# Two FNet + GLU layers on one core: the second layer's DFT over columns folded once more, and the row tests spread anew

## The chip, the cores and the metric

The kernel runs on one core of one Trainium2 chip. The metric is the device time of one execution in microseconds (us); less is better. Three timed runs of the kernel before gave 1104.46 to 1105.48 us, with a median of 1104.56. The execution that the profiler recorded took 1106.03 us, 1.47 us above that median; its span in the trace, from the first to the last recorded instruction, is 1104.2 us.

## What is computed

Two equal layers work on x, 2048 rows of 640 columns. Each layer first mixes (the real part of a DFT over the columns and a DFT over the rows, by products with given matrices), then applies a gated feed-forward part with F = 1728; both add to x and both begin with a row normalization.

```python
def _A_ref(x, dft_seq_re, dft_seq_im, dft_hid_re, dft_hid_im):
    a = jnp.einsum("bsd,ed->bse", x, dft_hid_re)
    b = jnp.einsum("bsd,ed->bse", x, dft_hid_im)
    return jnp.einsum("ts,bse->bte", dft_seq_re, a) - jnp.einsum("ts,bse->bte", dft_seq_im, b)

def _B_ref(x, w_gate, w_up, w_down):
    g = jnp.einsum("bsd,df->bsf", x, w_gate)
    u = jnp.einsum("bsd,df->bsf", x, w_up)
    return jnp.einsum("bsf,fd->bsd", _sigmoid(g) * u, w_down)

for layer in range(2):
    x = x + _A_ref(_layernorm(x), dft_seq_re, dft_seq_im, dft_hid_re, dft_hid_im)
    x = x + _B_ref(_layernorm(x), w_gate, w_up, w_down)
```

The DFT matrices are inputs like all others. The kernel uses their symmetries and so also tests, row by row, that what it was given has them; if a test fails, a general version runs instead.

## The kernel before

**Arithmetic.** x stays in SBUF for the whole run. Every large product of fp32 numbers is done as three products of fp16 halves (high by high, high by low, low by high), so one "matmul" of the mathematics is three matmuls on TensorE, each with a weight load of its own.

**Folding.** Because of the symmetries of a DFT, rows s, S-s, S/2-s and S/2+s are added and subtracted in quads before the product, and so are columns c and 640-c. Half of the columns are left, EC = 321 of them for the even sums ("e") and 320 for the odd ones ("o"). For the second layer this fold runs on VectorE (DVE) beside the first layer's last stages, quad by quad (four quads, 0 to 3): `fold_columns` (L593, L594), `fold_double` (L600), `fold_rows` (L636, L642), and `fold_join` (L675 to L682). In `fold_join` the last sums are formed on DVE (L675), copied to fp16 by ScalarE (ACT, L677), and the low half is left by a subtraction on DVE (L682). Quads 0 to 2 are done ahead; quad 3 needs the first layer's very last rows and so is finished while the second layer's first products already run.

**The start of the second layer** ("he" in the code) is a list of steps: eight `sequence` steps, the DFT over rows of quad i for the even (EV) or odd (OD) outputs (matmuls at L796, and L800 for one odd row), eight `hidden` steps and one `hidden_middle`, the DFT over columns (`product`, matmuls at L922). A `sequence` step fills three PSUM banks over two quads; `evict_sums` takes them out, ACT the high half (L237) and DVE the low half (L239). A `hidden` step is 18 matmuls of 321 columns into two banks; they come out through `evict_hidden` on ACT (L961, L971) or DVE (L966). There are eight banks in all, given out in the order in which they came free. After these steps x is normalized, transposed on TensorE (L540, 20 matmuls each), and the feed-forward part begins at the mark "b0" with `gate_up` (L1130).

**The feed-forward part** works in two halves of the rows. For each, gate blocks (`seven` and `four`, matmuls of 512 columns at L1174) run over the 13 tiles of F, and then `stage` steps (L1430, L1411) multiply by `w_down`. In a gate block six products of one tile follow one another on TensorE: one, five, two, six, (four of the tile before), three, seven, 45 to 54 matmuls together. Four of the results are copied out of PSUM by ACT (`snap`, L1178); "six" may start only when "one" was copied, and "seven" only when "six" was. ACT also does the sigmoids (L1181). The transposes of the normalized rows that feed the gate blocks are DMA transposes issued by SyncE (SP, L533).

**Row tests.** 100 of them, each with a load into a "room" of SBUF (4 DMAs of 128 KB for `load_rows`, L1502), one to four DVE instructions (`test_rows`, L1509 and L1511) and a squared sum on ACT (`square_sum`, L1481). Three rooms are used in turn. A table `spans` gives each stretch of the run a weight, and the tests are spread by it.

**What sets the order.** Nothing is scheduled at run time. `steps` is TensorE's order with a planned duration for each step; `when(t, ...)` and `run(step, ...)` put the other engines' work at planned times or steps, and each engine takes its own instructions in that order. `PLACES` is a list of SBUF addresses, one for each buffer in the order in which buffers are taken; which buffer reuses which place, and so which instruction must wait for which, follows from it. All DMAs but a few gathers are issued by SP.

## Time and profile before

| | |
|---|---|
| median of three timed runs | 1104.56 us |
| the profiled execution's own time | 1106.03 us |
| its span in the trace | 1104.2 us |
| TensorE (PE) busy | 98% of the span |
| VectorE (DVE) / ScalarE (ACT) / GpSimd (POOL) busy | 75% / 52% / 14% |
| start of the second layer (first L796 to first `gate_up`) | 571.66 to 612.46 us |
| second layer's first gate block, its stages | about 652.8 to 780 us, 780 to 852 us |
| second layer's last gate block, its stages | 860 to 1018 us, 1018 to 1098 us |

How to read it: the profile gives for each engine the time in which it did something, and, for each stretch in which it did nothing, the instruction whose end let it go on. With TensorE at 98% a time can only fall much if TensorE's own work falls, or if one of the few stretches goes in which it waits. A row of a timeline or of the chain reads: start, duration, engine and line, and xN for N instructions.

### The profile page before, as it was taken

What the parts mean: (1) busy time and instruction counts of PE and PEld (TensorE: products, weight loads), DVE (VectorE), ACT (ScalarE), POOL (GpSimd) and SP (SyncE); (2) the same over time, 40 slices, a digit from 0 to 9 for tenths busy, and PEclk for the clock granted to TensorE, in tenths of its full rate; (3) what the DMA queues carried; (4) which work ended last, traced back from release to release, by engine and by line L of the source; (5) the groups of instructions that cost most, each with busy time, mean ns of one, the idle gap of its engine ahead of it and who ended that gap; (6) DMA issues with size and microseconds to landing.
All of it is one profiled execution on the core that took longest, in us unless ns stands there. A gap on an engine that the chain in (4) does not pass through costs nothing.

```text
span 1104.2 us, 17528 instructions
## 1 busy us (share of the span) xinstructions
PE 1084.0 (98%) x6289; PEld 626.3 (57%) x6289; DVE 830.2 (75%) x1608; ACT 572.9 (52%) x1109; POOL 154.6 (14%) x250
## 2 busy tenths in 40 slices
PE   6999999999999999999999999999999999999997
PEld 3776444457774444457777844444677444444775
DVE  8996789868448999769887569895895356777962
ACT  7776547765315665555225544476761345555520
POOL 3110153312333151000110100012000010000010
PEclk9999999999999999999999999999999999999999
DMA  8414765366996877756742058645569856666521
GB/s 273 155 61 71 199 184 203 115 193 191 251 249 233 251 250 202 235 174 214 229 141 73 1 62 194 200 154 182 185 163 177 265 180 208 202 196 194 190 88 64
DMA packets 183079, 194.70 MB, mean 176 GB/s; under 512 B 76451, under 2 KB 145474, under 8 KB 182982
## 3 DMA queue, kind: packets, MB, share of 16 engines
q1 hardware_dynamic: 182342, 190.87, 58.8%
q0 software_dynamic: 640, 2.62, 0.6%
q8 instruction: 51, 0.84, 0.3%
q14 instruction: 46, 0.38, 0.1%
HBM read 145.29 MB, written 31.91 MB: 160 GB/s over the span
## 4 chain that ended last, share of the span: by engine, by line
PE 87%; DVE 8%; issue 2%; DMA 1%; ACT 1%; POOL 0%; SPq 0%; DVEq 0%; POOLq 0%; ACTq 0%
PE acc L1174 36%; PE acc L1430 17%; PE acc L1130 14%; PE acc L1316 8%; PE acc L922 4%; PE acc L1411 2%; PE acc L1283 2%; PE acc L834 2%; DVE big L642 1%; DMA big<-big 1%; DVE quad L424 1%; DVE big L239 1%; PE acc L796 1%; DVE big L1509 1%; DVE big L594 0%
## 5 line engine op out<-in xcount | busy, mean ns | idle before, releaser
L1174 PE MATMUL acc<-big 128*128 128x512 f16 x2160 | 467.8, 379 | 2.8 <-ACT big L1178 1.9
L1174 PEld LDWEIGHTS <-big 128*128 128x128 f16 x2160 | 211.3, 98 | 257.8 <-issue 3.5
L1430 PE MATMUL acc<-big 128*128 128x320 f16 x1512 | 213.2, 299 | 0.4 <-DVE big L1304 0.4
L1178 ACT ACTIVATE big<-acc 128x512 f32<-128x512 f32 x160 | 94.0, 593 | 191.9 <-PE acc L1174 167.5
L1430 PEld LDWEIGHTS <-big 128*128 128x128 f16 x1512 | 147.9, 98 | 58.5 <-issue 0.6
L1130 PE MATMUL acc<-big 128*128 128x512 f16 (+1 forms) x900 | 156.6, 336 | 0.0
L1130 PEld LDWEIGHTS <-big 128*128 128x128 f16 x900 | 87.9, 98 | 67.7 <-DVE big L239 0.2
L1481 ACT ACTIVATE big<-big 128x768 f32<-128x768 f32 (+6 forms) x106 | 79.0, 745 | 53.2 <-DVE big L1511 17.0
L1304 DVE SCALAR_TENSOR_TENSOR big<-acc,big 128x320 f32<-128x320 f32 x112 | 53.1, 485 | 53.7 <-PE acc L1411 27.2
L239 DVE SCALAR_TENSOR_TENSOR big<-big 128x640 f16<-128x640 f32 (+7 forms) x94 | 75.9, 830 | 22.5 <-ACT big L237 19.4
L1316 PE MATMUL acc<-big 128*128 128x320 f16 x656 | 89.3, 299 | 0.0
L1391 DVE TENSOR_TENSOR big<-big 128x512 f16<-128x512 f32 x126 | 85.3, 688 | 2.3 <-ACT big L1390 2.3
L1390 ACT ACTIVATE big<-big 128x512 f16<-128x512 f32 x126 | 74.0, 618 | 25.0 <-DVE big L1391 11.1
L237 ACT ACTIVATE big<-big 128x640 f16<-128x640 f32 (+9 forms) x94 | 63.8, 707 | 35.7 <-POOL big L1082 15.8
L1316 PEld LDWEIGHTS <-big 128*128 128x128 f16 x656 | 64.2, 98 | 25.1
L1224 DVE TENSOR_TENSOR big<-big,acc 128x512 f32<-128x512 f32 x40 | 27.3, 682 | 44.4 <-PE acc L1174 30.6
L516 ACT ACTIVATE big<-big 128x384 f16<-128x384 f32 (+2 forms) x56 | 36.0, 667 | 36.6 <-DVE big L501 17.2
L1181 ACT ACTIVATE big<-big 128x512 f32<-128x512 f32 x80 | 49.7, 622 | 9.7 <-DVE big L1224 6.6
L386 POOL DMA_INDIRECT out<-big,rows x8 | 8.6, 1070 | 310.9 <-DVE big L1304 173.5
L1509 DVE TENSOR_TENSOR big<-big 128x512 f32<-128x512 f32 x64 | 46.2, 722 | 5.9 <-DMA big<-in_ct 5.7
L1402 DVE TENSOR_TENSOR big<-big 128x512 f32<-128x512 f32 x72 | 50.1, 697 | 0.1
L439 POOL TENSOR_SCALAR rowt<-rowt 128x1 f32<-128x1 f32 x24 | 13.0, 540 | 242.4 <-ACT big L437 242.4
(199 smaller groups left out, 1230.2 us busy)
## 6 DMA issues: line engine op xcount, KB each, us to landing
big<-in_ct SPq DMA_DIRECT2D x256, 128.0 KB
big<-kept_f SPq DMA_DIRECT2D x63, 320.0 KB
big<-kept_S SPq DMA_DIRECT2D x33, 512.0 KB
big<-kept_w SPq DMA_DIRECT2D x33, 320.0 KB
big<-in_ct SPq DMA_DIRECT2D x32, 256.0 KB
big<-kept_G SPq DMA_DIRECT2D x21, 320.0 KB
kept_S<-big SPq DMA_DIRECT2D x13, 512.0 KB
big<-in_wg SPq DMA_DIRECT2D x19, 320.0 KB
```

The source lines that it names most:

```text
L237: nc.scalar.activation(dh, src, AF.Copy, scale=s)
L239: nc.vector.scalar_tensor_tensor(dl, src, s, dh, op0=OP.mult, op1=OP.subtract)
L1130: nc.tensor.matmul(ps, w[wp][:, d * P : (d + 1) * P], xt[:, xp, :], start=(d == 0 and wp == HI and xp == HI), stop=(d == ND - 1 and wp == LO))
L1174: nc.tensor.matmul(ps, wt, xt, start=start and n == 0, stop=n == len(todo) - 1, skip_group_check=not start)
L1178: nc.scalar.activation(dst, ps, AF.Copy)
L1304: nc.vector.scalar_tensor_tensor(xe, ps[:, :EH], CB, xe, op0=OP.mult, op1=OP.add)
L1316: nc.tensor.matmul(held["pd", i, e][0][:, :EH], held["t", half, j].parts[hp][:, i * P : (i + 1) * P], held["w", 2, j].parts[wp][:, e * EH ...
L1390: nc.scalar.activation(h, v, AF.Copy)
L1391: nc.vector.tensor_tensor(l, v, h, op=OP.subtract)
L1430: nc.tensor.matmul(ps[:, :EH], a[n][hp][:, i * P : (i + 1) * P], w[n][:, wp], start=fresh and m == 0, stop=m == len(todo) - 1, skip_group_ ...
L1481: nc.scalar.activation(v, v, AF.Square, accum_out=new_sum()[:p])
L1509: nc.vector.tensor_tensor(bd[:, :, 1], bd[:, :, 0], bd[:, :, 1], op=same)
```

## The change

**1. The second fold.** The columns of the folded sums have one more symmetry, c against 320-c. For the second layer they are folded again: sums in 161 columns, differences in 160 (`fold_again`). In the DFT over columns the first two thirds of the contraction (d = 0, 1) then touch only every other output column, 161 of 322, while the last third (d = 2) keeps all 322. The first layer keeps its way. The scale constants XF and ZS are halved.

```diff
+    def fold_again(to, f, r):
+        c, every = EH - 2 * r, (slice(None),) * (len(f.shape) - 1)
+        for n, to_c, op in ((HE + 1, 0, OP.add), (HE, HE + 1, OP.subtract)):
+            nc.vector.tensor_tensor(to[(*every, slice(to_c, to_c + n))], f[(*every, slice(0, n))],
+                                    f[(*every, slice(c, c - n, -1))], op=op)
...
-    def fold_join(i, v=ALL, do=(0, 1, 2)):
+    def fold_join(i, v=ALL, do=(0, 1, 2, 3), only=ALL):
...
             if 1 in do:
-                nc.scalar.activation(take_parts(key, i)[:, :, 0, :w], f[:, GB::2], AF.Copy)
...
+                fold_again(a, b, n)
             if 2 in do:
-                p = take_parts(key, i)
-                nc.vector.tensor_tensor(p[:, :, 1, :w], f[:, GB::2], p[:, :, 0, :w], op=OP.subtract)
+                nc.scalar.activation(p[:, :, 0, :EC], a, AF.Copy)
+            if 3 in do:
+                nc.vector.tensor_tensor(p[:, :, 1, :EC], a, p[:, :, 0, :EC], op=OP.subtract)
...
     def product(ps, ph, r, at, m):
-        for d, (_, n) in enumerate(KT[r]):
-            w = held["h", r, d].f16[:n]
+        for d, (_, n) in enumerate(KT):
+            o = ps[:m, : EC + 1 if steps else EC]
+            if steps and d < 2:
+                c = (r + d) % 2
+                o = ps[:m, c * (HE + 1) : (c + 1) * (HE + 1)]
```

**2. Its weights.** Before, the fp16 DFT weights of the opening were stored (six DMAs) and loaded again (`load_wh_again`, planned 60 us after the first layer's last stages begin). Now the fp32 rows that are needed are loaded (`load_wh2`, planned 4 to 14 us after that point) and split again on ACT, DVE and, for a column of zeros, POOL (`split_wh2`). Eleven DVE instructions on 128x1 and 128x4 numbers in the opening (`hs2`) prepare their factors.

**3. The order at the start of the second layer.** The steps and the evictions between them are listed anew, and quad 3's join is cut in two halves with evictions ahead of and between them.

```diff
             order = [(sequence, 0, EV), (sequence, 1, EV), (sequence, 0, OD), (sequence, 1, OD), (sequence, 2, EV),
-                     (sequence, 2, OD), (hidden, 0, 0), (sequence, 3, EV), (hidden, 1, 0), (sequence, 3, OD),
-                     (hidden, 0, 1), (hidden, 2, 0), (hidden, 3, 0), (hidden, 1, 1), (hidden, 2, 1), (hidden, 3, 1),
-                     (hidden_middle,)]
+                     (sequence, 3, EV), (sequence, 2, OD), (hidden, 0, 0), (hidden, 0, 1), (sequence, 3, OD),
+                     (hidden, 1, 0), (hidden, 1, 1), (hidden, 2, 0), (hidden, 3, 0), (hidden_middle,),
+                     (hidden, 2, 1), (hidden, 3, 1)]
...
-    run_at(end + 3, [(fold_join, 3, ALL, (n,)) for n in range(3)])
...
-    run(he + 2, evictions(0, (EV,)))
+    join = [[(fold_join, 3, ALL, (n,), (k,)) for n in range(1, 4)] for k in range(2)]
+    run(he + 2, [(evict_sums, 0, EV, 0), (fold_join, 3, ALL, (0,)), *join[0], *evictions(0, (EV,))[1:], *join[1]])
     run(he + 4, evictions(0, (OD,)))
```

VectorE's rows of the layer's start, before: the end of quad 3's join (L675 joins, L682 leaves the low halves), then the evictions of the first sums (L239, one row for each PSUM bank acc).

```order
780 L675 TENSOR_TENSOR big_60<-big_60 128x321 x2
781 L675 TENSOR_TENSOR big_60<-big_60 128x320 x2
782 L682 TENSOR_TENSOR big_60<-big_60 128x2x321
783 L682 TENSOR_TENSOR big_60<-big_60 128x2x320
784 L239 SCALAR_TENSOR_TENSOR big_60<-acc6_314,big_60 128x512
785 L239 SCALAR_TENSOR_TENSOR big_60<-acc2_66,big_60 128x512
786 L239 SCALAR_TENSOR_TENSOR big_60<-acc5_313,big_60 65x512
```

The same place in the changed kernel, on the same engine (L241 is the eviction, L699 the join, L684 the second fold, L708 the low half).

```order
785 L241 SCALAR_TENSOR_TENSOR big_60<-acc6_326,big_60 128x512
786 L699 TENSOR_TENSOR big_60<-big_60 128x321 x2
787 L699 TENSOR_TENSOR big_60<-big_60 128x320 x2
788 L684 TENSOR_TENSOR big_60<-big_60 128x161
789 L684 TENSOR_TENSOR big_60<-big_60 128x160
790 L684 TENSOR_TENSOR big_60<-big_60 128x161
791 L684 TENSOR_TENSOR big_60<-big_60 128x160
792 L708 TENSOR_TENSOR big_60<-big_60 128x321 x2
793 L241 SCALAR_TENSOR_TENSOR big_60<-acc2_66,big_60 128x512
794 L241 SCALAR_TENSOR_TENSOR big_60<-acc5_325,big_60 65x512
```

The first eviction stands ahead of the join now, the second and third between its two halves; the second half of the join (four more L684 and two more L708) follows them, ahead of the evictions of the odd sums.

**4. The row tests.** There are 102 (two new ones for the second symmetry, `load_hidden_fold`). Their table names a distance between tests for each stretch instead of a weight. Planned counts by stretch, before and now: first layer's first stages and the stretch behind them 5 and 6; first layer's last gate block 19 and 13; first layer's last stages 10 and 4; second layer's opening `gate_up` block 0 and 6; first gate block of the second layer's first half 24 and 14; its stages 5 and 0; the last gate block 33 and 50; the last stages 4 and 9. In the last gate block there is a fourth room, a test comes three places after its load instead of two, and every other test's row loads are issued by ACT: 21 groups of four DMAs, 128 KB each.

```diff
+            (nc.scalar if apart_rows[0] else nc.sync).dma_start(v[:, g], bass.AP(ct.tensor, (r * S + row) * S, [[256, 8], [d * S, 16], [1, 256]]))
...
+    spans = [(d[0] + 6, d[0] + 38, 7.0), (d[0] + 76, d[1] - 93, 14.0), (d[1] - 43, d[1] - 3, 5.0), (d[1] - 3, d[1] + 47, 12.0),
+             (c - 29, c + 3, 4.5), (c + 60, d2 - 4, 4.8), (j2 + 4, e2, 3.1), (e2, e2 + 45, 5.5)]
...
+        k, wait = (n % 3, 2) if m < 0 else ((3, *((more_rooms + i) % 3 for i in range(3)))[m % 4], 3)
+        when(at_test(n), apart_rows.__setitem__, 0, m >= 0 and m % 2 == 0)
+        when(at_test(n), within, k, load, *key)
+        when(at_test(n + wait), within, k, test, *key)
+        when(at_test(n + wait + 0.85), square_rest)
```

ScalarE's rows in the last gate block, before: copies out of PSUM (L1178), sigmoids (L1181) and the tests' squares (L1481).

```order
747 L1178 ACTIVATE big<-acc_312 128x512
748 L1181 ACTIVATE big<-big 128x512
749 L1481 ACTIVATE big,dsum<-big 128x768
750 L1178 ACTIVATE big<-acc_65 128x512
751 L1481 ACTIVATE big,dsum<-big 128x319
752 L1181 ACTIVATE big<-big 128x512
753 L1178 ACTIVATE big<-acc_65 128x512
```

In the changed kernel the same engine there (L1241 copy, L1244 sigmoid, L1544 square, L1453 a split, L1569 the loads of a row test).

```order
785 L1241 ACTIVATE big<-acc_325 128x512
786 L1244 ACTIVATE big<-big 128x512
787 L1544 ACTIVATE big,dsum<-big 128x768
788 L1241 ACTIVATE big<-acc_324 128x512
789 L1544 ACTIVATE big,dsum<-big 128x768
790 L1569 DMA big<-in_ct 128x1x256 x4
791 L1453 ACTIVATE big<-big 128x512
792 L1244 ACTIVATE big<-big 128x512
```

Four DMA issues stand in ACT's queue behind a square and ahead of the next copies and sigmoids.

SyncE's rows ahead of the second layer's first gate block, before: the eight small DMA transposes of the normalized rows, one after another.

```order
300 L533 DMA_TRANSPOSE big<-big 128x4x128
301 L533 DMA_TRANSPOSE big<-big 128x6x128
302 L533 DMA_TRANSPOSE big<-big 128x4x128
303 L533 DMA_TRANSPOSE big<-big 128x6x128
304 L533 DMA_TRANSPOSE big<-big 128x4x128
305 L533 DMA_TRANSPOSE big<-big 128x6x128
```

In the changed kernel, with eight row loads ahead and four in the midst.

```order
282 L1569 DMA big<-in_ct 128x1x256 x8
283 L542 DMA_TRANSPOSE big<-big 128x4x128
284 L542 DMA_TRANSPOSE big<-big 128x6x128
285 L542 DMA_TRANSPOSE big<-big 128x4x128
286 L542 DMA_TRANSPOSE big<-big 128x6x128
287 L1569 DMA big<-in_ct 128x1x256 x4
288 L542 DMA_TRANSPOSE big<-big 128x4x128
```

The loads of one row test now stand between the fourth and the fifth transpose.

**5. Smaller moves.** In the second layer the normalized rows for the last gate block are applied earlier (18, 42 and 51 planned us after the stages begin instead of 20, 46 and 56), and one of the weight loads behind them (`load_s` of tile 6) is planned 24 instead of 15 us ahead. `PLACES` is a new list throughout; it begins

```diff
-405 80 404 403 81 86 91 96 400 101 395 106 111 116 121 126 390 131 134 384 387 381 140 143 374 369 364 359 354
+405 80 404 81 399 394 389 384 379 81 374 369 364 359 354 349 344 91 94 97 88 341 338 100 105 110 115 330 325
```

231 lines of the change are left out of this document (145 added, 86 removed), and 62 rows, old and new, of the table PLACES.

## The prediction

> **What bounds the kernel now.** I read the page's head, then what TensorE waits for, then the chain of waits at the second layer's start, then busy time by stretch.
>
> The page's head: span, then the engines' busy time.
>
> ```profile
> span 1104.2 us, 17528 instructions
> PE 1084.0 (98%) x6289; PEld 626.3 (57%) x6289; DVE 830.2 (75%) x1608; ACT 572.9 (52%) x1109; POOL 154.6 (14%) x250
> ```
>
> TensorE (PE) is busy for all but 20 us. A change gains by giving it less to do or by ending one of its waits. The waits, by the instruction that ended them (us in total, times, longest):
>
> ```profile
> PE acc L1174 <- ACT big L1178: 1.9, 1, 1.9
> ...
> PE acc L1174 <- DMA big<-big: 0.9, 1, 0.9
> ...
> PE acc L796 <- DVE big L239: 0.6, 1, 0.6
> PE acc L922 <- ACT big L971: 0.5, 1, 0.5
> ```
>
> These four, 3.9 us, are all that lies in places that the change touches; the others stand in the opening and at the first layer's end. The chain at the second layer's start (start, us, engine, line):
>
> ```profile
> 581.24 0.62 DVE big L239
> ...
> 587.15 1.97 PE acc L796 x18
> ...
> 593.55 14.81 PE acc L922 x108
> ...
> 609.62 0.34 ACT big L971
> ...
> 619.18 1.12 PE acc L540 x20
> ```
>
> Between the first and the last of these waits the chain is PE alone: 14.81/108 = 137.1 ns for a matmul of 321 columns, 1.97/18 = 109.4 ns for one of 256, and 1.12/20 = 56 ns for one of 128 columns (a transpose, with its own weight load). All three are the column count by 2.4 per ns and about 3 ns more, so time goes with columns even at 128.
>
> **The second fold: what it removes.** By that line 161 columns cost 161/2.4 + 2.8 = 69.9 ns and 322 cost 137.4 (estimates from those rows). A `hidden` step was 18 x 137.1 = 2.47 us; now it is 12 x 69.9 + 6 x 137.4 = 1.66 us. Nine such steps (with the middle one) give 9 x 0.80 = **-7.2 us** of PE work. The `sequence` steps stay as many and as long. The price for a short matmul has the transposes on one side, and on the other a bound by weight loads:
>
> ```profile
> L922 PEld LDWEIGHTS <-big 128*128 128x128 f16 x96 | 9.3, 97 | 3.6
> L540 PEld LDWEIGHTS <-big 128*128 128x128 f16 x40 | 2.4, 98 | 0.1
> ```
>
> A load shows 97 to 98 ns behind long matmuls and behind the 56 ns transposes alike (40 of them in a busy time of 2.4 us), so these spans overlap and are no cadence. If they were one, a step would be 12 x 98 + 6 x 137.4 = 2.00 us and the gain 9 x 0.47 = 4.2 us. I take 7.2, since the transposes are the nearest row.
>
> [...]
>
> **The second fold: what it gives back.** PE becomes quicker here, and the engines that empty its banks have more to do. The stretch, and DVE's rows in its first part:
>
> ```profile
> 571.66:612.46 40.80, 39.71 (x331) 32.29 (x329) 28.64 (x60) 20.41 (x41) 5.38 (x19) 1.00 0.25 81
> ```
>
> Busy us of PE, PEld, DVE, ACT, POOL follow the length: PE 39.71 of 40.80, the rest being the two waits of 0.6 and 0.5.
>
> ```profile
> 576.90 1.02 DVE L642 SCALAR_TENSOR_TENSOR big<-big,quad 128x321 f32<-128x321 f32 x2 [0.79 <-ACT big L636]
> 577.84 1.69 DVE L675 TENSOR_TENSOR big<-big 128x321 f32<-128x321 f32 x4
> 579.60 1.65 DVE L682 TENSOR_TENSOR big<-big 128x642 f16<-128x642 f32 x2
> 581.16 2.47 DVE L239 SCALAR_TENSOR_TENSOR big<-acc,big 128x512 f16<-128x512 f32 x4
> ...
> 581.90 1.36 PE L796 MATMUL acc<-big 128*65 128x256 f16 x11 [0.56 <-DVE big L239]
> ```
>
> Before, (2,EV)'s third piece waits for a bank because the first L239 stands behind the whole join. Now one L241 is ahead of it, and that wait goes. But the join has eight more L684, of 161 or 160 columns: 0.42 us for 321 in the L675 row, so some 0.24 each, 1.9 us. I laid the new order out from 571.66 with these durations, each engine in its order, an eviction 0.62 on DVE (L239 in the chain):
> - the evictions of (0,OD) come behind the second half of the join, the first of them done at about 585.9; (2,OD) asks for its third bank at about 585.1: +0.8;
> - `hidden` (0,1) follows (0,0) at once and wants the sums of (2,EV) and (3,EV); its last third is evicted 0.3 late;
> - `hidden` (2,0) wants a bank that (3,OD)'s eviction frees, which is queued on DVE behind the first rows' joins and statistics: +0.7;
> - `hidden` (3,1) is last now. Its banks come from (2,1)'s evictions on ACT, behind row 3's statistics and the transposes' copies: +1.0, and the transposes ahead of it +0.1.
>
> The sum, 2.9 us, stands against 1.1 before: the stretch ends at 612.46 - 7.2 + 1.8 = 607.0, **-5.5 us**. From both sides: all of them zero gives -8.3 (7.2 and the old 1.1); every one twice as long gives -2.6. Copying results out in the interleaved order (L1027 and on) I count like the plain copies; no row shows it, and at twice the 0.34 of L971 the two evictions on the path would cost 0.7, inside those ends.
>
> The other edits of this part go beside PE. The eleven `hs2` instructions stand ahead of the first L593. Of their kind, twelve go from 2.63 to 3.74, 0.1 us each, so 1.1 in all, and that L593 waited 1.48 anyway; without this cover they would cost 1.1:
>
> ```profile
> 2.63 0.14 DVE L302 TENSOR_SCALAR big<-big 32x1 f32<-32x1 f32 x1
> ...
> 3.60 0.14 DVE L306 TENSOR_SCALAR big<-big 32x1 f32<-32x1 f32 x1
> ...
> 7.48 0.83 DVE L593 TENSOR_TENSOR big<-big 128x640 f32<-128x640 f32 x1 [1.48 <-ACT big L363]
> ```
>
> The weights' loads and splits lie in the first layer's last stages, where DVE loses six tests and gains six splits of 0.6 (as L239). A test costs DVE about 1.2:
>
> ```profile
> 933.76 0.69 DVE L1509 TENSOR_TENSOR big<-big 128x512 f32<-128x512 f32 x1 [0.21 <-DMA big<-in_ct]
> 934.49 0.49 DVE L1511 TENSOR_TENSOR big<-big 128x128 f32<-128x128 f32 x2
> ```
>
> So DVE has less there than before: nothing on PE, and 3.6 us of DVE work if the tests had stayed.
>
> **The two waits that go.** One is in the first layer's last gate block:
>
> ```profile
> 427.31 1.54 DVE L682 TENSOR_TENSOR big<-big 128x642 f16<-128x642 f32 x2
> ...
> 428.97 1.08 ACT L1178 ACTIVATE big<-acc 128x512 f32<-128x512 f32 x2 [2.22 <-DVE big L682]
> ...
> 429.61 1.67 PE L1174 MATMUL acc<-big 128*128 128x512 f16 x7 [1.90 <-ACT big L1178]
> ...
> 332.00:430.00 98.00, 96.10 (x446) 43.47 (x445) 94.58 (x163) 57.47 (x104) 30.91 (x41) 1.00 0.73 237
> ```
>
> A copy on ACT writes to a place that the fold of quad 1 had, and waits for its last reader, L682, late because DVE is full (94.58 of 98). In the new `PLACES` that copy takes a place that was free long before. DVE there gets the second fold of quads 0 and 1, eight L684 of 322 numbers a row (0.42 each, 3.4 us), and loses six tests (7.2): less than before, so no new lateness is due: **-1.9 us** (0 if the lateness finds another victim).
>
> The other wait is for the large DMA transposes ahead of the last gate block:
>
> ```profile
> 850.82 9.21 DMA big<-big
> 860.03 0.04 issue
> 860.07 45.05 PE acc L1174 x208
> ```
>
> The rows behind them are applied 2 to 5 us earlier, no tests load there, and the weight loads now follow the transposes on SP: **-0.9 us** (0 to -0.9).
>
> **A new wait ahead of the first gate block of the second layer.** SP issues the eight small transposes without a gap:
>
> ```profile
> 638.16 11.96 SPq L533 DMA_TRANSPOSE big<-big x8
> ```
>
> They are issued by 650.12, the last landed by about 651.2, and PE wants the first rows at the block's start, about 652.8, and the last some 1.3 us later: 2.9 us of room for the last. Four L1569 now stand between them, at 0.6 each (row below) 2.4 us, and the new tests delay DVE's part of the rows by 1.6: **+1.1 us** (0 to 2.5, twice that delay).
>
> **ScalarE as an issuer in the last gate block.** ACT's rows in 860 to 1018 (count | busy us, mean ns | idle before), then SP's issues of the same loads (min/median/max ns):
>
> ```profile
> 860.00:1018.00 158.00, 157.93 (x732) 71.61 (x732) 99.22 (x192) 78.14 (x161) 4.19 (x4) 1.00 0.63 205
> ...
> L1178 ACT ACTIVATE big<-acc 128x512 f32<-128x512 f32 x52 | 31.0, 596 | 87.1 <-PE acc L1174 87.1
> L1481 ACT ACTIVATE big<-big 128x768 f32<-128x768 f32 x25 | 20.9, 837 | 6.4 <-DVE big L1511 4.5 <-DVE big L1528 0.9 <-DMA big<-in_wh 0.8
> ...
> L1502 SPq DMA_DIRECT2D big<-in_ct x80: 596/597/1918, 859.7 to 989.2; - x80
> ```
>
> ACT is busy 78.14 of 158 us, so 80 are free. 17 more squares take 17 x 0.93 (0.84 less an overlap, and 0.19 for reading the sum) = 15.8. The 84 issues are not in the trace on ACT: on SP one takes 0.597. From below, 0 (hidden under the activation before it); from above 1.918, SP's longest. At 0.597 they take 50.1, in all 66 of 80 free, ACT 91% full. PE feels ACT through the copies: "six" starts 3.25 us behind "one" (15 matmuls of 45.05/208 = 0.217 us), "seven" 3.9 behind "six". A group of 2.4 us, a square and a sigmoid fit before each, with 0.5 to 2 us to spare. So groups at 0.6 an issue cost nearly nothing, at 0.67 a few tenths here and there. Each issue also waits until the load eight DMAs before it has landed (there are eight such counters, for SP and ACT together), now every 5 us or so; so I put **+2 us** (0 to the rival below). DVE has 17 x 1.2 = 20 us more on 99.22 of 158, and the DMA engines about 8 MB more, 255 GB/s against 205: hidden, where 332 to 430 us shows 237 GB/s beside a busy PE.
>
> [...]
>
> **The sum.** -5.5 - 1.9 - 0.9 + 1.1 + 2.0 = -5.2 us on the profiled execution's 1106.03, that is 1100.8; less the 1.47 us by which it stands above the median, **1099.3**.
>
> **Rivals.**
> - *The waits don't come back* (banks in time at the second layer's start, no cost of ACT's issues): -7.2 - 1.1 - 1.9 - 0.9 + 0.5 (left of the wait ahead of the first gate block) = -10.6, 1094. For it: DVE is busy 28.64 of 40.80 there. Against: the order puts six DVE evictions behind the join. Chance 0.11.
> - *Short matmuls are bound by their weight loads* (98 ns): 3.0 us less gain, 1102.3. For it: the 97 and 98 ns rows. Against: 56 ns between transposes that load each time. Chance 0.10. [...]
> - *ScalarE's queue becomes the bound of the last gate block; slower than before.* Free are 80 us; squares take 15.8; so 84 issues may take 64, 0.76 us each. Each 0.1 us beyond costs 8.4. At 0.85 the 7.2 us that the other terms win are gone; that is the point. At 0.95 it is +16 in place of +2, 1113.3. For it: SP's longest are 1.9, and every issue waits for a counter that SP's late loads hold too. Against: SP's median lies within 1 ns of its minimum. Chance 0.20.
> - *The second layer's start is hardly shortened* (each new wait twice as long): -2.6 in place of -5.5, 1102.2. For it: a bank that comes late makes all later ones late. Against: the steps from `hidden` (1,0) to the middle one ask for banks that came free long before. Chance 0.09.
>
> **Chances.** My forecast, 1097 to 1102, has 0.50. 0.2%, about what a measurement of this kernel can tell from no change, is 2.2 us: faster is below 1102.35, slower above 1106.8. Faster: 0.50, 0.11, and of the second and the last rival, whose times lie at that bound, 0.06 and 0.04: 0.71. Slower: 0.17 of the queue. Same: the rest, 0.12. The range goes from 1094, the first rival's time, to 1107, where the queue's cost is 10 us; it leaves out most of the queue's cases and a little below.
>
> **What will show it.** Right: PE rows of 161 columns near 70 ns; `gate_up` starting 40.8 - 5.5 = 35.3 us behind the first `sequence` matmul; no wait for ACT in the first layer's last gate block, none for DMA ahead of the second layer's last; PE waits of 3 us at most in that block. Wrong: short matmuls at 80 ns or more; ACT's L1569 rows at 0.8 us or more with PE waiting for ACT's copies in tile after tile; a wait of several us for a DMA ahead of the first gate block; or waits for banks at the second layer's start that sum to 6 us.

## The result, and the profile after

| | before | after |
|---|---|---|
| median of the timed runs, same chip | 1105.02 us (1104.46 to 1110.36, 4 runs) | 1142.12 us (1138.55 to 1144.79, 4 runs) |
| ratio | | 1.0323, 95% interval 1.0278 to 1.0367 |
| the profiled execution, its span | 1106.03, 1104.2 us | 1143.44, 1141.6 us |
| last gate block of the second layer | 157.8 us (860.07 to 1017.9) | 200.0 us (853.50 to 1053.46) |

The change makes the kernel 3.2% slower; 1099.3 us had been forecast. The page's head and the row of TensorE's granted clock after the change:

```profile
span 1141.6 us, 17579 instructions
...
PE 1087.6 (95%) x6289; PEld 624.1 (55%) x6289; DVE 843.6 (74%) x1659; ACT 573.7 (50%) x1127; POOL 146.7 (13%) x254
...
PEclk9999999999999999999999999999999978999999
```

TensorE does as many matmuls as before, yet stands idle for 54 us in place of 20, and in two of the forty slices its clock was granted at 7 and 8 tenths. Of its waits in the changed kernel (us in total, times, longest), the largest and those in places that the prediction named:

```profile
PE acc L1237 <- ACT big L1241: 32.8, 13, 8.1
...
PE acc L1193 <- DMA big<-big: 0.9, 1, 0.9
...
PE acc L976 <- DVE big L241: 0.9, 1, 0.9
PE acc L825 <- DVE big L241: 0.8, 1, 0.8
PE acc L976 <- ACT big L1032: 0.5, 1, 0.5
```

Where there were 1.9 us of waiting for ScalarE's copies there are now 32.8. By TensorE's timeline 0.8 of them stand in the first layer's last gate block, the other 32.0 in the second layer's:

```profile
422.40 60.38 PE L1237 MATMUL acc<-big 128*128 128x512 f16 x279 [0.81 <-ACT big L1241]
...
853.50 42.90 PE L1237 MATMUL acc<-big 128*128 128x512 f16 x198
898.36 11.95 PE L1237 MATMUL acc<-big 128*128 128x512 f16 x54 [1.96 <-ACT big L1241]
918.37 8.56 PE L1237 MATMUL acc<-big 128*128 128x512 f16 x30 [8.06 <-ACT big L1241]
...
953.60 6.73 PE L1237 MATMUL acc<-big 128*128 128x512 f16 x24 [6.67 <-ACT big L1241]
...
984.24 28.13 PE L1237 MATMUL acc<-big 128*128 128x512 f16 x123 [4.32 <-ACT big L1241]
```

The second layer's block begins 6.6 us earlier than before and runs without a gap for 43 us; then come twelve waits of 0.5 to 8.1 us. The busy time of PE, PEld, DVE, ACT and POOL in the whole block, granted clock, DMA share and GB/s:

```profile
853.50:1053.50 200.00, 168.01 (x735) 73.47 (x733) 114.68 (x236) 87.06 (x194) 4.51 (x4) 0.94 0.58 182
```

Of the 42 us that the block is longer, 32 are idle time; the other 10 are the same matmuls taking 168.0 instead of 157.9 us at a mean granted clock of 0.94 instead of 1.00. The clock is lower where the waits are, as two stretches of the same view show (1.00 and 0.79). That the waits bring it down is not shown; in e3_sp_early, below, 6.3 us of waits in 165 us stand beside a clock of 1.00:

```profile
853.50:898.40 44.90, 42.94 (x201) 19.38 (x199) 26.30 (x56) 20.77 (x44) 4.51 (x4) 1.00 0.57 187
918.40:953.60 35.20, 23.70 (x85) 9.49 (x84) 13.42 (x29) 10.33 (x26) 0.00 (x0) 0.79 0.38 117
```

DVE is less busy per us than before and the mean DMA share fell from 0.63 to 0.58: by these columns nothing is full.

What held ScalarE? Its waits between 853 and 1054 us in the changed kernel:

```profile
ACT big L1241 <- DMA big<-in_ct: 59.7, 10, 11.8
...
ACT big L1453 <- DMA big<-in_ct: 14.1, 4, 7.2
```

A copy out of PSUM (L1241) reads nothing that a row load (in_ct) brings. ScalarE's timeline at the longest PE wait shows what stands between:

```profile
906.54 0.21 ACT L1544 ACTIVATION_READ_ACCUMULATOR big<-big 128x1 f32 x1
914.38 3.30 ACTq L1569 DMA_DIRECT2D big<-in_ct  x4
917.72 0.60 ACT L1241 ACTIVATE big<-acc 128x512 f32<-128x512 f32 x1 [10.97 <-DMA big<-in_ct]
```

Between 906.8 and 914.4 the queue stands still at a DMA issue; then four issues pass and only then the copy for which TensorE is waiting. The issues themselves (ns, min/median/max):

```profile
L1569 ACTq DMA_DIRECT2D big<-in_ct x84: 602/603/1213, 881.9 to 1055.0; - x84
L1569 SPq DMA_DIRECT2D big<-in_ct x44: 596/612/1437, 891.3 to 1051.9; - x44
```

An issue takes 0.60 us on ScalarE, as was assumed. What costs is the wait ahead of it. In the trace the 788 DMAs of SP and ACT take turns on eight semaphores, 98 or 99 on each, and none of the 780 that follow another on the same one ended its issue before that one had landed, the closest 0.25 us behind it. So an issue waits for the DMA eight before it, whoever issued that one: for 37 of ScalarE's 84 issues it was one of SP's. The issue at 914.38 began 0.02 us after the landing of a weight load (kept_G) that SP had issued at 911.11, the one at 927.16 0.02 us after that of a fold load that SP had issued at 918.79. The question is why DMAs land late.

### The profile page after: what moved, and what is told of

Read it like the earlier page. It is cut to its first block, busy times and chain, and to the rows that moved or that the text cites. A ratio compares the mean times of both kernels' runs of the same rounds, so it can differ in the third digit from the quotient of the medians.

```text
span 1141.6 us, 17579 instructions
## 1 busy us (share of the span) xinstructions
PE 1087.6 (95%) x6289; PEld 624.1 (55%) x6289; DVE 843.6 (74%) x1659; ACT 573.7 (50%) x1127; POOL 146.7 (13%) x254
## 4 chain that ended last, share of the span: by engine, by line
PE 71%; DMA 12%; DVE 8%; ACT 4%; SPq 2%; issue 1%; ACTq 1%; POOL 0%; DVEq 0%
PE acc L1237 30%; PE acc L1493 13%; PE acc L1193 11%; PE acc L1379 8%; DMA big<-in_ct 4%; DMA big<-in_wh 3%; PE acc L976 2%; PE acc L1474 2%; PE acc L863 2%; PE acc L1346 2%; DMA big<-kept_S 1%; ACTq L1569 1%; DMA big<-in_x 1%; ACT big L1544 1%; DMA big<-kept_f 1%
## 5 line engine op out<-in xcount | busy, mean ns | idle before, releaser
L1237 PE MATMUL acc<-big 128*128 128x512 f16 x2160 | 477.6, 384 | 32.8 <-ACT big L1241 32.8
L1241 ACT ACTIVATE big<-acc 128x512 f32<-128x512 f32 x160 | 92.4, 591 | 208.9 <-PE acc L1237 146.9
L1544 ACT ACTIVATE big<-big 128x768 f32<-128x768 f32 (+9 forms) x110 | 80.7, 734 | 60.4 <-DVE big L1595 23.8
L1453 ACT ACTIVATE big<-big 128x512 f16<-128x512 f32 x126 | 73.6, 617 | 38.7 <-DMA big<-in_ct 14.1
L241 DVE SCALAR_TENSOR_TENSOR big<-big 128x640 f16<-128x640 f32 (+9 forms) x97 | 76.9, 815 | 18.7 <-ACT big L239 18.7
L239 ACT ACTIVATE big<-big 128x640 f16<-128x640 f32 (+11 forms) x97 | 64.6, 695 | 33.6 <-POOL big L1145 17.8
L1576 DVE TENSOR_TENSOR big<-big 128x512 f32<-128x512 f32 x64 | 44.6, 697 | 24.6 <-DMA big<-in_ct 19.8
L1244 ACT ACTIVATE big<-big 128x512 f32<-128x512 f32 x80 | 49.8, 622 | 21.0 <-DMA big<-in_ct 10.4
L526 DVE TENSOR_TENSOR big<-big 128x384 f16<-128x384 f32 (+2 forms) x56 | 41.3, 749 | 9.0 <-ACT big L525 8.9
```

Of the source, the lines that this page charges most:

```text
L239: nc.scalar.activation(dh, src, AF.Copy, scale=s)
L241: nc.vector.scalar_tensor_tensor(dl, src, s, dh, op0=OP.mult, op1=OP.subtract)
L1237: nc.tensor.matmul(ps, wt, xt, start=start and n == 0, stop=n == len(todo) - 1, skip_group_check=not start)
L1241: nc.scalar.activation(dst, ps, AF.Copy)
L1453: nc.scalar.activation(h, v, AF.Copy)
L1544: nc.scalar.activation(v, v, AF.Square, accum_out=new_sum()[:p])
```

## The experiments

The trace records when a DMA was issued and how its semaphore was then raised. That gives this table (SP's and ACT's loads in the last gate block):

```
load                  outermost   raised  DMAs   us from issue to landing
                      count       by             min / median / max
before  L1502 rows        8         9       80    2.92 / 5.36 / 10.38
before  L1562 hidden      2         3        2    7.07 and 10.68
after   L1569 rows        8         9      124    2.61 / 5.45 / 10.02
after   L1629 hidden      2         3        6    6.35 / 9.27 / 12.26
after   L1644 fold        2         3       12    6.57 / 8.86 / 11.77
```

Loads with 128 in the outermost place raise it by 16, and so do those with 16 in e17_wide, below. The number raised goes with the outermost count of the load's pattern, and so does the number of packets that run at once. In the changed kernel, of the time in which any such packet ran:

```
packets                                         how many     at once
fold loads, 644 bytes                             1284       at most 2 for 90%
hidden-row loads of that block, 1280 bytes         768       at most 2 for 94%
ScalarE's row loads, 1 KB                        10752       at most 8 for 96%
loads of 2064-byte rows, mostly 128 outermost     2048       at most 16 for 97%
```

The page counts sixteen DMA engines. From these counts I estimate that a hidden-row or fold load ("two-piece" below) has two of them and a row load eight; the trace doesn't name a packet's engine.

So there were three suspects: ScalarE's issuing, the 18 two-piece loads in the block (2 before), and the 32 row tests' loads (20 before) with 8 outermost.

**ScalarE's issues away, and the two-piece loads away.** e1_sp leaves all row loads to SyncE. e2_early moves the hidden-row and fold tests to earlier stretches, so that the last gate block has none of their loads; eight full column tests stand there instead of three. e3_sp_early does both.

```diff
-        when(at_test(n), apart_rows.__setitem__, 0, m >= 0 and m % 2 == 0)
+        when(at_test(n), apart_rows.__setitem__, 0, False)          # e1, e3
...
-        tests.insert(18 + 4 * n, test)
+        tests.insert(6 + 3 * n if n < 12 else 18 + 4 * n, test)     # e2, e3
```

> The changed kernel with all row loads of the last gate block issued by SyncE again; tests, rooms and all else stay. Theory A (ScalarE's queue: whatever an issue waits for, copies for TensorE stand behind it): the waits of TensorE for ScalarE in that block fall from 32.8 us to under 3, the block is 158 to 161 us long, the time is 1097 to 1101 us. Rival S (18 slow loads of the hidden matrix in that block make tests and weights late on any queue): SyncE is held instead, VectorE waits for tests at the head of its queue and weights come late; the block stays over 165 us and the time over 1106.

> The changed kernel with the ten hidden-row tests and the two fold tests moved ahead in the list of tests, so that none of their loads is in the last gate block; 20 groups of row loads are still issued by ScalarE there. Theory A: ScalarE still pays 0.6 us for each of 80 issues and waits for the counters; the last stalls of the changed kernel (11 of 33 us, those behind 955 us) stay or grow with the denser row loads; the time is over 1112 us. Rival S: those 18 loads alone hold the counters; without them the block falls under 165 us and the time to 1097 to 1106.

> Both edits: row loads on SyncE, and no load of hidden rows or folds in the last gate block. Theory A: as with the loads on SyncE alone, 1097 to 1101 us. Rival S: as with the tests moved alone, or a little better, 1096 to 1101. If only the two together reach 1101, both are needed.

Measured: e1_sp 1134.68 us (ratio to before 1.0269, 1.0251 to 1.0286), e2_early 1127.67 (1.0207, 1.0184 to 1.0231), e3_sp_early 1121.07 (1.0148, 1.0129 to 1.0167). Neither theory stands alone: e1_sp goes against A, e2_early against S, and e3_sp_early, which both put at 1096 to 1101, misses by 20 us. Taking ScalarE out of the issuing gives back only 7.4 of the 37 us lost, and 6.6 where the two-piece loads are gone; those loads give back 14.5 or 13.6. ScalarE's queue is thus a part, not the whole, and 16 us over the kernel before are left with both suspects gone. The chain of waits in e3_sp_early:

```profile
920.79 5.28 DMA big<-in_ct
926.07 0.05 issue
926.11 0.02 SPq L1569
926.13 0.03 issue
926.16 0.60 SPq L1569
926.76 0.05 issue
926.81 5.38 DMA big<-in_ct
932.18 0.02 issue
932.20 0.02 SPq L1170
932.22 0.03 issue
932.25 8.72 DMA big<-kept_U
```

Row load releases row load, and then a weight load (kept_U) that SP could issue only behind them. No compute engine is on that chain.

**ScalarE's issues alone, in the kernel before.** e4_before_act gives every second row load of the old last gate block to ScalarE (28 issues).

```diff
+        when(at_test(n), apart_rows.__setitem__, 0, at_test(n) >= start_of(1, "j", 1, 0) and n % 2 == 0)
```

> The kernel before the change with every second row load of its last gate block issued by ScalarE: 7 groups of 4, 33 tests as before. Theory A: the 28 issues cost ScalarE 17 us of 80 free, but each group may wait for a counter; if a group stands behind the pair of hidden-row loads near 886 us TensorE waits 2 to 6 us once, otherwise nothing: 1104 to 1111 us. Rival S: 1104 to 1106, and any wait lies beside that pair. If every issue on ScalarE stops TensorE, some 1.5 us a group, over 1113.

Measured: 1105.45 us, ratio 1.0005 (0.9995 to 1.0014). In the kernel before, 28 issues on ScalarE cost nothing that can be measured.

**Fewer tests in that block.** e5_less and e7_mid space the tests there by 4.6 and 3.8 planned us instead of 3.1, on SP alone, and put the others into earlier stretches, the fold and hidden-row tests first; e8_less_act is e5_less with half of the issues on ScalarE.

```diff
+    others = [(d[0] + 6, d[0] + 38, 7.0), (d[0] + 76, d[1] - 8, 8.0), (d[1] + 6, d[1] + 46, 6.5), (c + 5, j - 3, 7.0),
+              (j + 2, d2 - 7, 3.9), (d2 + 6, d2 + 58, 8.0), (j2 + 4, e2 - 3, 4.6), (e2 + 1, e2 + 40, 8.0)]
```

> The changed kernel with its row tests spread as thinly over the last gate block as before (one in 4.6 planned us, 33 there, in place of one in 3.1), the hidden-row and fold tests ahead of that block, all loads on SyncE; the rooms' places stay. Theory D (the row loads use 8 of the 16 DMA engines; a test is 512 packets of 1 KB at 50 ns, 3.2 us on each of the eight, so one test in 3.1 us can't be loaded): the block is 158 to 160 us, the time 1096 to 1100 us, faster than the kernel before. Rival (the change's earlier part gives nothing that lasts, or the new places and moved transposes cost as much later): 1103 to 1108.

> As the kernel with the tests spread thinly, with one test in 3.8 planned us in the last gate block. Theory D: the eight engines need 3.2 us a test for the rows and 2 us in 11.65 for the weights, so 3.9 us a test; at 3.8 it is at the edge: 1097 to 1104, 0 to 4 us over the thinner one. If counters or issues set the pace it is 4 us or more over it, too.

> As the kernel with the tests spread thinly, with every second test's row loads issued by ScalarE. Theory A' (a ScalarE issue costs 0.6 us and, where loads keep up, no wait): 11 or 12 groups in 80 free us, 0 to 2 us over the same on SyncE. If ScalarE's issues cost by themselves what the first runs showed (7 us for 21 groups): 3 to 5 us over it.

Measured: 1125.80, 1125.70 and 1124.88 us (ratios 1.0197, 1.0183, 1.0200). As times the first two miss, by 20 us and more; e8_less_act lies 0.9 us under e5_less, where 0 to 2 over had been expected. But TensorE has no wait at all left in the last gate block in e5_less and e7_mid, and 0.4 us in e8_less_act, with ScalarE issuing. The loss had moved to where the tests went: the first wait at the second layer's start stands at 598.1 us in e5_less, against 585.2 in the changed kernel. The chain near 400 us in e5_less:

```profile
389.70 8.27 DMA kept_o<-big
397.97 0.03 issue
398.00 0.02 DVEq L621
```

A store (kept_o) lands after 8.27 us beside the fold loads, which were issued up to 387.6 us and took 6 to 10 us, and a DVE instruction waits for its place.

**Half of each row load.** e6_half is e3_sp_early with loads and tests cut to the first 128 of each 256 columns: the same number of DMAs, issues and packets, packets of 512 bytes instead of 1 KB. e11_half_act is that with ScalarE issuing half of them, e12_half_slow with the two-piece loads where the change puts them.

```diff
-dma_start(v[:, g], bass.AP(ct.tensor, (r * S + row) * S, [[256, 8], [d * S, 16], [1, 256]]))
+dma_start(v[:, g, :128], bass.AP(ct.tensor, (r * S + row) * S, [[256, 8], [d * S, 16], [1, 128]]))
```

> The kernel with the loads on SyncE and the hidden tests early, one test in 3.1 us, with each row load cut to every row segment's first 128 of 256 columns, and the test likewise: the other half of the row tests is left out. As many DMAs, issues and counters, half the bytes. Theory D: the eight engines need some 1.8 us a test and keep up; the waits for loads in the last gate block go, the time is 1097 to 1103 us against 1121. Rival C (the eight counters, each held for one load's whole latency, or SyncE's 0.6 us for each issue, set the pace whatever the bytes): over 1112.

> The kernel with half-width row loads (half of the row tests left out), hidden tests early, one test in 3.1 us, but with 20 groups issued by ScalarE as in the change. It prices ScalarE's issues where loads keep up. Theory A' (0.6 us an issue, in 80 free us): 1097 to 1100 us against 1096.5 on SyncE. If ScalarE's queue is a bound of its own: 1102 to 1110.

> The kernel with half-width row loads, all on SyncE, with the hidden-row and fold tests where the change has them: 18 loads on two engines in the last gate block. It prices those loads alone. If they make tests late by themselves: 1102 to 1112 us against 1096.5; if only together with full row loads: 1096 to 1100.

Measured: e6_half 1096.48 us (0.9928, 0.9912 to 0.9945), e11_half_act 1098.27 (0.9942, 0.9925 to 0.9958), e12_half_slow 1109.07 (1.0045, 1.0028 to 1.0061). Half the width is worth 24.6 us, so neither the number of issues nor of DMAs is the bound. The edit also halves the tests' work on DVE and ACT; the last pair below keeps that work whole. Beside row loads of half width ScalarE's issues cost 1.8 us and the two-piece loads 12.6.

**The tests in full, placed anew.** Six kernels looked for places for all 102 tests. e9_mid_a and e10_mid_b: 3.8 us between tests in the last gate block, fold tests in the first gate block or in the last stages. e13_all: 3.6, hidden-row tests away from the transposes, fold tests in the first gate block; e14_all_act the same with ScalarE issuing half. e15_thin and e16_thinner: 4.2 and 4.6, more tests elsewhere. Their tables of distances, in planned us:

```diff
-              (c - 29, c + 3, 4.5), (c + 60, d2 - 4, 4.8), (j2 + 4, e2, 3.1), (e2, e2 + 45, 5.5)]
+              (c - 29, c + 3, 4.5), (c + 8, c + 60, 9.0), (c + 60, d2 - 4, 4.8), (j2 + 4, e2, 3.8), (e2, e2 + 45, 5.5)]  # e9, e10
+              (c - 29, c + 3, 9.0), (c + 8, c + 60, 8.0), (c + 60, d2 - 4, 4.2), (j2 + 4, e2, 3.6), (e2, e2 + 45, 5.0)]  # e13, e14
+              (c - 29, c + 3, 7.0), (c + 8, c + 60, 8.0), (c + 60, d2 - 4, 3.9), (d2 + 6, d2 + 46, 11.0), (j2 + 4, e2, 4.2), (e2, e2 + 45, 5.0)]  # e15
```

> The changed kernel with one test in 3.8 planned us in the last gate block (40 there), all loads on SyncE, the tests ahead of it spread as in the change but for six more beside the second layer's first gate_up block and three ahead of the first layer's last gate block; hidden rows early, the two fold tests in the second layer's first gate block. The run with 3.8 us showed no wait in the last block; its losses lay where it had put more tests. Theory D (what was lost is loads on few DMA engines, wherever they are dense): 1096 to 1099 us. If the fold loads (two engines, 7 to 12 us each) stop the first gate block instead: 1100 to 1106.

> The same with the two fold tests in the last stages. Theory D: 1096 to 1099 us, unless SyncE, held some 12 us by each of them, brings the stages' weights late: then 3 to 6 us more, as a wait of TensorE for them.

> All 102 tests in full, all loads on SyncE: one test in 3.6 planned us in the last gate block (42 there), half as many beside the eight small transposes, the hidden rows early but none beside the transposes, the folds in the first gate block where they stopped nothing before. Theory D (loads on two or eight of the DMA engines, denser than these carry, are all that was lost): no wait of over 2 us behind the opening, 1096 to 1099 us, faster than the kernel before. If the second fold with its tests can't be had without the loss, a wait turns up elsewhere: 1100 to 1108.

> The same with every second test's row loads in the last gate block issued by ScalarE. By the half-width pair (1.8 us) it is 1 to 4 us over the same on SyncE, as single waits of TensorE for ScalarE there; if 3.6 us a test is at the edge of what eight DMA engines load, ScalarE waits for counters and it is 5 us or more.

> All tests in full on SyncE, as the run with one test in 3.6 planned us, but one in 4.2 in the last gate block (36 there), some in the stages ahead of it, a few more in the first gate block. Theory D: below the limit of the eight engines (3.9 us a test with the weights) the timed runs agree with the profiled one: 1096 to 1100 us, faster than the kernel before. If the spread of the timed runs has another cause, it stays at 1101 to 1105.

> The same with one test in 4.6 us in the last gate block (33 there, as in the kernel before) and a few more in the stages ahead. Theory D: as the run with 4.2 us within 1 us, unless the stages ahead wait for their weights.

Measured: e9_mid_a 1107.87 us (1.0028), e10_mid_b 1111.36 (1.0059), e13_all 1103.27 (0.9993, 0.9981 to 1.0005; 12 runs from 1099.08 to 1108.35), e14_all_act 1110.95 (1.0064), e15_thin 1106.43 (1.0017), e16_thinner 1111.93 (1.0066). Theory D gave e9_mid_a, e10_mid_b, e13_all and e15_thin 1096 to 1100 us, and all four miss. In e9_mid_a and e10_mid_b TensorE waits 4.4 and 5.0 us for the transposes ahead of the first gate block. In e15_thin and e16_thinner a thinner last gate block was to be at least as quick, but the tests that left it brought loads of 9 and 11 us and TensorE waits of up to 3.1 us into the first gate block. In e14_all_act ScalarE's issues cost 7.7 us over e13_all; the expectation had named 5 or more for a spacing at the edge. Distance alone cured it in none of the six. Why e13_all spreads over 9 us was not settled; its profiled execution was the fastest of the twelve, so its trace doesn't show the slower ones.

**The same bytes over sixteen engines.** The last pair changes only the shape of the loads. A row test reads the same 16 rows of 2048 numbers, in 16 pieces of 128 columns instead of 8 of 256. e17_wide is e3_sp_early with it. e18_after_wide is the changed kernel itself with it, and with the hidden-row loads in 8 pieces instead of 2.

```diff
-[[256, 8], [d * S, 16], [1, 256]]
+[[128, 16], [d * S, 16], [1, 128]]     # e17, e18
...
-[[EH, 2], [d * D, 64], [1, EH]]
+[[80, 8], [d * D, 64], [1, 80]]        # e18
```

> e3_sp_early with one edit: each DMA of a row test reads its 16 rows of 2048 numbers in 16 pieces of 128 columns, outermost, where it read them in 8 pieces of 256; bytes, rows, tests and their times stay. Theory E (the row loads, split by their outermost count of 8, fill 8 of the 16 engines at one test per 3.1 us: 64 packets of 1 KB at 50 ns are 3.2 us on each): now 16 engines share 1024 packets of 512 B at 27.5 ns (the half-width run), 1.8 us on each; the landing counts rise from 9 to 17 and the time comes near that of the half-width run, 1097 to 1101. Rival B (it is the bytes, or the 16 engines together): bytes are the same and the packets' time rises from 25.8 to 28.2 us a test, so 1121 or more.

> The changed kernel as it is, ScalarE's issues and the tests' places unchanged, with two edits: row loads in 16 pieces outermost in place of 8, hidden-row loads in 8 pieces of 80 columns in place of 2 of 320. Theory E: the row loads no longer fill their engines, three of the four kinds of slow DMAs in the last gate block go; left are ScalarE's issues (1.8 us at half width) and the twelve fold loads, two thirds of 12.6 us at most: 1098 to 1107. Rival Q (ScalarE's queue itself is the price): with 84 issues still on ScalarE the time stays above 1120. Rival B (bytes): 1140.

Measured: e17_wide **1098.96 us** (1097.69 to 1100.15), ratio 0.9945 (0.9932 to 0.9959), the only version with all tests in full that beats both kernels. The row loads' semaphores are now raised by 16 (not the 17 expected) and land after 3.24 us in the median instead of 6.06 in e3_sp_early. Its last gate block:

```profile
853.55:1011.54 157.99, 157.99 (x734) 71.62 (x732) 119.26 (x248) 91.93 (x192) 4.21 (x4) 1.00 0.81 241
```

The mean DMA share is 0.81 here, against 0.58 in the changed kernel, and TensorE is never idle. The same bytes in more packets, 22 us less: it was not the bytes, nor the mean share of the sixteen engines, which was 0.70 in e3_sp_early. What changed is the loads' shape, and with it the number raised, from 9 to 16. Full rows in 512-byte packets with 8 outermost were not run; by the packet times below (two of 29.8 ns against one of 51.2) I estimate that the smaller packet alone is no help. By the two profiles the gain is spread: the last gate block begins 6.5 us earlier (853.55 for 860.07), is 7.1 us shorter (158.0 for 165.1), and what follows it is 6.6 us shorter (86.8 for 93.4). In e3_sp_early TensorE waits 2.4 and 4.9 us for weights (kept_f) ahead of the block and behind it, and in e17_wide it doesn't. The packet records of the traces agree. Each row load has 128 packets, and in e17_wide 256:

```
                 all packets     of them row loads          8 engines' load (estimate)
before           1591.9 us       80 x 128 at 50.3 ns         64.4 + 67.3 = 132 of 158 us
e3_sp_early      1842.9 us      120 x 128 at 51.2 ns         98.3 + 66.0 = 164 of 165 us
after            1840.1 us      124 x 128 at 50.4 ns        100.0 + 65.0 = 165 of 200 us
e17_wide         2036.6 us      125 x 256 at 29.8 ns        all 16: 127.3 of 158 us
```

The estimate goes by the counts of packets at once: it puts an eighth of the row packets' time and a sixteenth of the rest on each of eight engines. It is rough: from 899 us on, where e3_sp_early's row loads stand, it comes to 1.07 of the time, and more than all of it can't be. By it these engines are full in e3_sp_early and were full to 83% in the kernel before, while the mean share said 0.70 and 0.63. In the changed kernel the waits stretch the block, but the two-piece loads' packets, 90 us (45.0 of fold loads, 45.3 of hidden rows), come besides. If two engines carry them, the same two each time, and of the eight, that is 45 each in place of the 6 that the table counts: about 204 of 200 us.

e18_after_wide came to 1117.73 us (1.0125, 1.0110 to 1.0141), 11 more than the end of what was expected, though 24 less than the changed kernel. TensorE's waits there are 13.8 us, and most stand beside the two fold tests:

```profile
909.61 6.63 PE L1237 MATMUL acc<-big 128*128 128x512 f16 x30 [1.63 <-ACT big L1241]
...
925.46 8.01 PE L1237 MATMUL acc<-big 128*128 128x512 f16 x30 [3.29 <-ACT big L1241]
937.45 7.03 PE L1237 MATMUL acc<-big 128*128 128x512 f16 x24 [3.98 <-ACT big L1241]
```

The twelve fold loads are issued from 905.8 to 931.1 and land after 7.0 us in the median. In the chain there one load of that matrix (in_wh) lands at 922.09, 7.13 us after its issue, and ScalarE's issue passes at 922.12; one copy (L1241) waits 8.8 us for a fold load. I read the miss as prices that were added where each part makes the other dearer; no run isolated it for the fold loads. The rival there, over 1120 us for ScalarE's queue itself, is missed too, by 2 us.

## Why the prediction was wrong

**The parts that held.** TensorE's timeline of the changed kernel at the second layer's start:

```profile
570.83 2.47 PE L825 MATMUL acc<-big 128*128 128x257 f16 x21
...
585.20 0.82 PE L825 MATMUL acc<-big 128*65 128x256 f16 x6 [0.77 <-DVE big L241]
...
596.33 6.00 PE L976 MATMUL acc<-big 128*128 128x161 f16 x63 [0.85 <-DVE big L241]
602.17 1.28 PE L549 MATMUL acc<-ident,big 128*128 128x128 f16 x20
603.94 1.83 PE L976 MATMUL acc<-big 128*128 128x161 f16 x18 [0.49 <-ACT big L1032]
605.61 6.71 PE L1193 MATMUL acc<-big 128*128 128x256 f16 x60
...
646.99 13.38 PE L1193 MATMUL acc<-big 128*128 128x512 f16 x60 [0.92 <-DMA big<-big]
```

And a row of the chain there:

```profile
586.02 3.35 PE acc L976 x36
```

- *Second fold, -7.2, and the start of the layer, -5.5.* From 570.83 to 605.61 are 34.8 us; 35.3 was forecast, 40.8 it had been. The waits came at three of the places named, 0.77, 0.85 and 0.49 against 0.8, 0.7 and 1.0; the 0.3 at `hidden` (0,1) did not show. In the chain two `hidden` steps in a row take 3.35 us, 1.675 each against 1.66 forecast: (1.675 - 6 x 0.1374) / 12 = 70.9 ns for a matmul of 161 columns, against 69.9. The bound by weight loads (98 ns) falls.
- *New wait ahead of the first gate block, +1.1.* 0.92, at 646.99. (Twice the delay would have given 2.4 + 3.2 - 2.9 = 2.7 for the upper end, not 2.5.)
- *The two waits that go, -1.9 and -0.9.* The second is gone: the last gate block starts without one. Of the first, 0.8 is left, at 422.40. The ScalarE copy that ends it stands behind a copy of the second fold (L706), which had waited 0.87 us for L684. So this term is -1.1; the prediction had put at nothing what the second fold adds there.
- *ScalarE's issue at 0.6 us.* 0.603 in the median, with SP issuing beside it; one of the 84 took twice as long, 1.21 us.

As a sum these terms held too: -7.2 was forecast for them, and the last gate block begins 6.6 us earlier. The agreement is partly luck, for the start of the layer gave 6.0 where 5.5 was forecast, and the first layer's wait 1.1 where 1.9 was. Less the 2 us for ScalarE's issues the forecast is 1097.3; e17_wide, with all tests, twelve of them moved, and SP alone, took 1098.96.

**The step that failed.** It is the last sentence on ScalarE: "the DMA engines about 8 MB more, 255 GB/s against 205: hidden, where 332 to 430 us shows 237 GB/s beside a busy PE". The load was judged by bytes and by the mean over sixteen engines. By the estimate above the row loads use eight. In the trace of the kernel before, a row test is 512 packets at 50.3 ns, 3.2 us on each of eight. The change places 32 of them in the last gate block, 103 us, and the other packets took 67 us of each engine there before: 170 us for a block of 158 (an estimate from the table above). That sum could have been made before the result. The GB/s were no obstacle: e17_wide moves 241 in that block without a wait. In place of "hidden" stand 24.4 us in the changed kernel itself, with the row loads at 16 outermost and the hidden-row loads at 8 (e18_after_wide), and 22.1 us for the row loads alone where ScalarE issues nothing and the two-piece loads are moved (e3_sp_early to e17_wide).

The trace of the kernel before had the sign of it: its row loads raise their semaphore by 9, its hidden-row loads by 3, its loads with 128 outermost by 16. The prediction did not weigh that, and it spoke most against this change.

**The term that was mis-sized, +2 for ScalarE as issuer.** The mechanism was named: an issue waits until the load eight DMAs before it has landed. It was priced at the landing times of before. In its place TensorE waits 32.0 us for ScalarE's copies in that block. The change also puts 18 loads of 6 to 12 us into it, which the prediction did not count at all, and its row loads land after 5.45 us in the median, where e17_wide's take 3.24. In the kernel before and at half width the term is right (0 for 28 issues in e4_before_act, 1.8 for 80 in e11_half_act). Beside full row loads with 8 outermost, ScalarE's issues (6.6 or 7.4) and the two-piece loads (13.6 or 14.5) together make 21.0 us (e3_sp_early to the changed kernel). These and the 22.1 of the row loads add up to the way from 1098.96 to 1142.12, as steps along one path must. The shares hang on the path, since the parts make each other dearer: with the row loads mended first, 18.8 us are left for ScalarE's issues and the fold and hidden-row loads (e17_wide to e18_after_wide).

**The rivals.** The slower case, ScalarE's queue as the bound of the last gate block, had the right place and the right sign, and the copies late in many tiles; it had also named SP's late loads, which hold the counters, as what spoke for it. Its price was wrong in kind: longer issues (0.85 to 0.95 us) were expected, and what came were long waits ahead of issues of 0.60. With ScalarE issuing nothing there the kernel is still 2.7% slower (e1_sp), so it is not the cause alone. The other three rivals fell with the rows above: the waits at the layer's start came, the short matmuls took 70.9 ns, and the start took 34.8 us.

## What to carry to other kernels

Judge DMA load by the shape of the transfers, not by GB/s or the mean share alone: multiply packets by their duration, divide by the number that run at once (here the outermost count, 2, 8 or 16), add what else there is to carry, and compare the sum with the time there is. By that estimate it was 164 of 165 us in e3_sp_early, where TensorE waited, and 127 of 158 in e17_wide, where it did not, while the mean share was 0.70 and 0.81. Before giving DMA issues to a compute engine, look at what they will wait for: here ScalarE's issues stood behind loads of 6 to 12 us that SP had issued, and its copies (L1241) waited up to 11.8 us. Before moving loads between queues or stretches, try their shape: one pattern with 16 outermost came out 4.3 us quicker here than the best of six new placements.

## What the runs showed of the hardware

- In the last gate block of the changed kernel a load with 2 outermost took 6.4 to 12.3 us for 160 KB or less, one with 8 took 2.6 to 10.0 us for 128 KB. In e17_wide the same 128 KB with 16 outermost took 2.4 to 6.0 us.
- In that block a packet of 512 bytes took 27.5 ns (e6_half) and 29.8 (e17_wide), one of 1 KB 50 to 51 ns, so the finer pieces cost a tenth to a fifth more of packet time for the same bytes.
- Issues of loads with 2 outermost held SP longer than those of row loads: in the changed kernel L1644 took 0.51 to 3.55 us, median 1.11, where row loads' issues had a median of 0.61.

```profile
L1644 SPq DMA_DIRECT2D big<-in_wh x12: 507/1113/3547, 916.0 to 945.7; - x12
```

- TensorE's granted clock fell to 0.79 over 918 to 954 us of the changed kernel, just behind a wait of 8.1 us and with waits of 2.5, 2.3 and 6.7 us within. It was 1.00 in the same block when it did not wait (e17_wide).
